# A decode kernel's output path: rows replicated over 32 partitions, halves merged by a predicated copy, and a finer last weight load

## The chip, the cores and the metric

The kernel runs on one core of one Trainium2 chip. The metric is device time in microseconds (us). A kernel is compared only with runs of the kernel before on the same chip in the same rounds. Engines are named as in the profile: PE (matmul), PEld (weight load), DVE (VectorE), ACT (ScalarE), POOL (GpSimd), SP (the queue that issues nearly all DMAs).

Two measures must be kept apart when reading on. A *time* (402.97 us) is the device's own, a *span* (401.6 us) is from the first to the last instruction of the one profiled execution.

## The reference, cut to what matters

One token is decoded. Part A is attention with 32 query heads over 4 key and value heads with 65,536 cached positions each. Part B is an MLP with four weight matrices. Both add to the same 1024 outputs.

```python
x  = A_x                                   # (1, 1, 1024), bf16
xn = _layernorm(x)
return x + _A_ref(xn, k_cache, v_cache, wq, wo) + _B_ref(xn, w1, w2, w3, w4)
# _A_ref: softmax(q k^T) v over 65536 positions, then @ wo
# _B_ref: ... h2 = gelu(layernorm(x1) @ w3) @ w4   (w4 is 3584 x 1024); x1 + h2
```

The caches and the weights are 170 MB, each byte is read once, and there is little to compute on each.

## The kernel before

SBUF is allocated in order of declaration. The small tensors come first, then four large ones: `W`, `Kn` and `Vn` receive the DMAs, `X` receives DVE transposes.

```python
orow = sb("orow", [P, 256], BF)            # output row, 512 bytes a partition
W  = sb("W",  [P, 14336], BF)              # weights
X  = sb("X",  [P, 2, 8192], BF)            # transposed K, written by DVE, read by PE
Kn = sb("Kn", [P, 2, 16384], BF)           # K cache, wq, at the end w4
Vn = sb("Vn", [P, 2, 16384], BF)           # V cache, wq, a part of wo
```

The output is summed in one PSUM tile. Its 1024 columns lie as four segments of 256 on partitions 0, 32, 64 and 96. A stationary operand of one column gives one row per segment, and four matmuls at four tile positions run side by side (in the trace one takes up to 0.42 us, and sixteen together take 1.02 us).

```python
def out_rows(items, reads, last=False):
    fns = []
    for lhs, rhs in items:                 # one weight row each
        for jj in range(4):
            fns.append(lambda e, ...: e.matmul(
                OUT_ps[32 * jj:32 * jj + 1, 0:256], lhs, rhs[:, 256 * jj:256 * jj + 256],
                start=False, stop=last, tile_position=(0, 32 * jj), ...))
    _grp(q_pe, fns, reads=reads, writes=[b_OUT], partial=True)
```

`_grp` makes PE wait for whoever wrote `OUT_ps` last. At the end the weight w4 arrives in four parts. Each entry is first row, number of rows, slot and offset; a row is 2 KB on each of 128 partitions.

```python
w4_parts = [(0, 14, 0, 0), (14, 8, 1, 0), (22, 4, 1, 8), (26, 2, 0, 14)]
...
for i in range(len(w4_parts)):
    w4_pe(i)                               # waits for part i, then 4 matmuls a row
_op(q_dve, lambda e: e.tensor_copy(orow[:, :], OUT_ps[:, 0:256]), ...)
ev_out = _dma(q_sp, ..., out=out[0, 0, :].rearrange("(j n) -> j n", j=4), in_=orow[0:97:32, :])
```

## Time and profile before

| Quantity | Value |
|---|---|
| time, median | 402.97 us |
| span of the profiled execution | 401.6 us |
| DMA | 170.20 MB at 424 GB/s, busy 0.9 or more in 38 of 40 slices |
| DVE, PE busy | 57%, 47% |
| last weight data packet ends | 398.39 us |
| last landing (completion of the last load) | 398.76 us |
| last output matmul ends | 399.42 us |
| store issued, span ends | 399.90 us, 401.59 us |

These lines of the page of the kernel before give the DMA's busy share in tenths and its rate over 40 slices, then its packets.

```profile
DMA  8999999999999999999999999999999999999995
GB/s 353 431 416 433 447 421 419 447 436 421 441 441 420 419 441 437 424 434 436 428 426 444 436 421 428 442 434 427 424 450 418 439 441 424 421 428 431 437 420 217
DMA packets 7088, 170.20 MB, mean 424 GB/s; under 512 B 916, under 2 KB 920, under 8 KB 1048
```

The DMA engines never rest until the last slice. Work on PE, DVE, ACT or POOL costs nothing while the stream hides it.

The chain of waits of the kernel before, at its end (start in us, duration in us, what):

```profile
374.88 23.88 DMA Kn<-in_B_w_dram
398.76 0.04 issue
398.80 0.62 PE OUT_ps L391 x7
399.42 0.02 issue
399.45 0.42 DVE orow L618
```

The timeline of the same stretch (start, duration, engine, line, operation, count, and in brackets the idle time before it and what ended it):

```profile
397.58 1.02 PE L391 MATMUL OUT_ps<-Kn,gh_bf 128*1 128x256 bf16 x16 [0.50 <-DMA Kn<-in_B_w_dram]
398.80 0.60 PE L391 MATMUL OUT_ps<-Kn,gh_bf 128*1 128x256 bf16 x8 [0.20 <-DMA Kn<-in_B_w_dram]
399.45 0.42 DVE L618 CAST orow<-OUT_ps 128x256 bf16<-128x256 f32 x1 [11.34 <-PE OUT_ps L391]
399.90 0.65 SPq L619 DMA_DIRECT2D out_dram<-orow  x1
```

PE begins the last eight matmuls 0.04 us after the last landing. From there it is a chain of latencies to the end of the span.

### The profile page before, as it was taken

To read this page: it belongs to the slowest core of one execution; us is meant where nothing else is said; L and a number is where in the kernel's file an instruction comes from. 1 tells how busy PE (TensorE), PEld (TensorE's weight loads), DVE (VectorE), ACT (ScalarE), POOL (GpSimd) and SP (SyncE) were. 2 spreads that over 40 slices of the span, in tenths; PEclk is the share of its full clock that TensorE was granted. 3 is DMA by queue.
4 is the path that set the end of the run, shared out by engine and by line. 5 is a ranking of instruction groups with operands and counts; after the bars stand their busy time and mean duration, and the time that the engine had idled before them with its cause. 6 is when DMAs were issued, how large, how long until landed. Compare 5 with 4: busy or idle time off the path is not lost.

```text
span 401.6 us, 5142 instructions
## 1 busy us (share of the span) xinstructions
PE 187.7 (47%) x2043; PEld 84.2 (21%) x2059; DVE 227.8 (57%) x400; ACT 48.4 (12%) x127; POOL 62.0 (15%) x90
## 2 busy tenths in 40 slices
PE   0361445064525745275630966353433545344674
PEld 0250111021103511062110731121111311111142
DVE  0217666277806588255753387676836775778410
ACT  0000211011101011011110011111201111112100
POOL 5000013011211011110310102111110102122110
PEclk9999999999855565555565555665565855656556
DMA  8999999999999999999999999999999999999995
GB/s 353 431 416 433 447 421 419 447 436 421 441 441 420 419 441 437 424 434 436 428 426 444 436 421 428 442 434 427 424 450 418 439 441 424 421 428 431 437 420 217
DMA packets 7088, 170.20 MB, mean 424 GB/s; under 512 B 916, under 2 KB 920, under 8 KB 1048
## 3 DMA queue, kind: packets, MB, share of 16 engines
q1 hardware_dynamic: 6920, 169.87, 98.4%
q8 instruction: 16, 0.26, 0.2%
q14 instruction: 8, 0.07, 0.0%
q10 hardware_dynamic: 144, 0.00, 0.0%
HBM read 169.87 MB, written 0.00 MB: 423 GB/s over the span
## 4 chain that ended last, share of the span: by engine, by line
DMA 54%; DVE 24%; PE 17%; issue 2%; ACT 2%; another core or an unknown queue 1%; SPq 0%; POOL 0%; ACTq 0%
DMA Kn<-in_A_k_cache_dram 43%; DVE X L463 12%; DMA Kn<-in_B_w_dram 6%; DMA Vn<-in_A_wq_dram 5%; PE H_ps L366 4%; DVE pT_f L516 3%; PE S_ps L475 3%; PE OT_ps L523 3%; DVE mrow L482 3%; PE M_ps L366 2%; ACT p_sb L505 2%; PE PT_ps L514 1%; PE M_ps L551 1%; PE OUT_ps L391 1%; DVE Yall L380 1%
## 5 line engine op out<-in xcount | busy, mean ns | idle before, releaser
L463 DVE STREAM_TRANSPOSE X<-Kn 128x1024 f32<-128x1024 f32 x128 | 151.7, 1215 | 64.5 <-DMA Kn<-in_A_k_cache_dram 64.5
L523 PE MATMUL OT_ps<-Vn,pT_f 128*32 128x512 bf16 x512 | 59.9, 620 | 54.1 <-DVE pT_f L516 54.1
L475 PE MATMUL S_ps<-X,Yall 128*32 128x512 bf16 x512 | 58.0, 598 | 17.0 <-DVE X L463 17.0
L488 PE MATMUL MB_ps<-Rm,Lmat 128*128 128x16 bf16 x32 | 6.2, 193 | 87.7 <-DVE Rm L483 87.7
L537 POOL TENSOR_TENSOR O_acc<-O_acc,tmpO 128x513 f32<-128x513 f32 x28 | 32.9, 1176 | 89.1 <-ACT tmpO L531 89.1
L535 POOL TENSOR_SCALAR O_acc<-O_acc,ff 128x513 f32<-128x513 f32 x28 | 19.6, 700 | 150.7 <-ACT ff L510 150.7
L505 ACT ACTIVATE p_sb<-S_ps,brun 128x512 bf16<-128x512 f32 x32 | 22.0, 688 | 173.1 <-DVE brun L503 154.6
L482 DVE TENSOR_REDUCE mrow<-S_ps 128x1 f32<-128x512 f32 x32 | 21.6, 674 | 24.6 <-PE S_ps L475 24.6
L531 ACT ACTIVATE tmpO<-OT_ps 128x512 f32<-128x512 f32 x32 | 19.2, 598 | 107.8 <-PE OT_ps L523 107.8
L475 PEld LDWEIGHTS S_ps<-X,Yall 128*32 128x32 bf16 x512 | 16.5, 126 | 54.7 <-DVE X L463 38.6
L516 DVE STREAM_TRANSPOSE pT_f<-PT_ps 128x512 f32<-128x512 f32 x32 | 22.9, 716 | 7.8 <-PE PT_ps L514 4.2
L523 PEld LDWEIGHTS OT_ps<-Vn,pT_f 128*32 128x32 bf16 x512 | 14.6, 128 | 59.4 <-DVE pT_f L516 42.7
L488 PEld LDWEIGHTS MB_ps<-Rm,Lmat 128*128 128x128 bf16 x32 | 3.3, 103 | 112.2 <-DVE Rm L483 112.2
L514 PE MATMUL PT_ps<-p_sb,permR 128*128 128x512 bf16 x16 | 9.5, 594 | 21.2 <-ACT p_sb L505 21.2
L366 PEld LDWEIGHTS H_ps<-xn_bf,W 128*128 128x128 bf16 x224 | 14.4, 172 | 1.7 <-issue 1.7
L366 PE MATMUL H_ps<-xn_bf,W 128*128 128x1 bf16 x224 | 14.5, 202 | 0.0
L514 PEld LDWEIGHTS PT_ps<-p_sb,permR 128*128 128x128 bf16 x32 | 3.4, 106 | 42.4 <-ACT p_sb L505 42.4
L492 DVE TENSOR_REDUCE Bst<-MB_ps 128x1 f32<-128x16 f32 x32 | 5.6, 174 | 8.3 <-PE MB_ps L488 8.3
L330 PE MATMUL M_ps<-ln_s,ones_f 128*128 128x1 f32 x6 | 1.8, 362 | 17.5 <-DVE ln_s L329 17.5
L533 POOL COPY O_acc<-tmpO 128x513 f32<-128x513 f32 x4 | 2.5, 615 | 47.5 <-ACT tmpO L531 47.5
L551 PE MATMUL M_ps<-O_acc,cb_W 128*128 128x128 f32 x32 | 7.4, 403 | 2.0 <-DVE cb_W L544 2.0
L391 PE MATMUL OUT_ps<-Kn,gh_bf 128*1 128x256 bf16 x112 | 5.8, 370 | 3.5 <-DMA Kn<-in_B_w_dram 3.5
(101 smaller groups left out, 114.0 us busy)
## 6 DMA issues: line engine op xcount, KB each, us to landing
Kn<-in_A_k_cache_dram SPq DMA_DIRECT2D x15, 4096.0 KB, 27.4
Vn<-in_A_v_cache_dram SPq DMA_DIRECT2D x15, 4096.0 KB, 22.3
W<-in_B_w_dram SPq DMA_DIRECT2D x2, 3584.0 KB, 25.1
W<-in_A_wo_dram SPq DMA_DIRECT2D x3, 2048.0 KB, 23.2
Kn<-in_A_wq_dram SPq DMA_DIRECT2D x1, 4096.0 KB, 12.3
Vn<-in_A_wq_dram SPq DMA_DIRECT2D x1, 4096.0 KB, 21.4
W<-in_B_w_dram SPq DMA_DIRECT2D x2, 2048.0 KB, 32.2
Kn<-in_A_k_cache_dram SPq DMA_DIRECT2D x2, 2048.0 KB, 24.8
```

The costliest lines, as they stand in the source:

```text
L366: fns.append(lambda e, j=j, cx=cx: e.matmul(ps_tile[:, c0 + cx:c0 + cx + 1], lhs_fn(j - j0, cx), rhs_fn(j), start=(j == 0 and cx == 0), st ...
L463: _op(q_dve, lambda e, ix=ix: e.transpose(out=X32[:, xs, 1024 * ix:1024 * (ix + 1)], in_=Kn32[:, s, 4096 * half + 1024 * ix:4096 * half + ...
L475: fns.append(lambda e, we=we, cm=cm, mv=mv: e.matmul(S_ps[32 * cm:32 * cm + 32, :], Yall[:, h, we, :, :].rearrange("p a g -> p (a g)"), mv ...
L482: _op(q_dve, lambda e: e.reduce_max(mrow[:, m:m + 1], S_ps[:, :], axis=AX.X), reads=[b_S], writes=[b_mrow[m]])
L505: _op(q_act, lambda e: e.activation(p_sb[:, m, :], S_ps[:, :], ACTF.Exp, bias=brun[:, kn:kn + 1], scale=SCALE, accum_out=tmpO[:, m, 512:513]),
L514: _op(q_pe, lambda e: e.matmul(PT_ps[:, :], permR[:, :], p_sb[:, m, :], start=True, stop=True), reads=[b_p[m], b_const], writes=[b_PT])
L516: _op(q_dve, lambda e: e.transpose(out=pT_f[:, :], in_=PT_ps[:, :]), reads=[b_PT], writes=[b_pT])
L523: fns.append(lambda e, q=q, q4=q4: e.matmul(OT_ps[32 * q4:32 * q4 + 32, :], pT_bf[:, q, :, 1], Vn[:, s, 8192 * half + 512 * q:8192 * half ...
L531: _op(q_act, lambda e: e.activation(tmpO[:, m, 0:512], OT_ps[:, :], ACTF.Copy), reads=[b_OT], writes=[b_tmpO[m]], partial=True)
L535: _op(q_pool, lambda e: e.tensor_scalar(out=O_acc[:, :], in0=O_acc[:, :], scalar1=ff[:, m:m + 1], scalar2=0.0, op0=ALU.mult, op1=ALU.add), ...
L537: _op(q_pool, lambda e: e.tensor_tensor(out=O_acc[:, :], in0=O_acc[:, :], in1=tmpO[:, m, :], op=ALU.add), reads=[b_tmpO[m]], writes=[b_Oacc])
L551: fns.append(lambda e, t=t: e.matmul(M0_ps[:, 128:256], cb_W[:, t, :, :].rearrange("p g i -> p (g i)"), O_acc[:, t * P:(t + 1) * P], start ...
```

## The change

The change is meant to shorten that tail. Loading the last two weight rows one by one should leave four matmuls behind the last landing, not eight. A stationary operand broadcast to 32 columns puts each output segment on all 32 partitions of its quadrant. Then partitions 0 to 15 can keep the first 128 columns of a segment and partitions 16 to 31 the second 128, by a plain copy and a predicated copy, and the store has eight rows of 256 bytes in place of four of 512.

```diff
-        orow = sb("orow", [P, 256], BF)
+        orow = sb("orow", [P, 128], BF)
+        omask = sb("omask", [P, 1], F32)
...
+        _op(q_dve, lambda e: e.reduce_sum(omask[:, 0:1], sel16[...][:, :, 2:4], axis=AX.XY), ...)
...
-   OUT_ps[32 * jj:32 * jj + 1, 0:256], lhs, rhs[:, 256 * jj:256 * jj + 256],
+   OUT_ps[32 * jj:32 * jj + 32, 0:256], lhs.broadcast_to([P, 32]), rhs[:, 256 * jj:256 * jj + 256],
...                                        # the same in out_resid
-        w4_parts = [(0, 14, 0, 0), (14, 8, 1, 0), (22, 4, 1, 8), (26, 2, 0, 14)]
+        w4_parts = [(0, 14, 0, 0), (14, 8, 1, 0), (22, 4, 1, 8), (26, 1, 0, 14), (27, 1, 0, 15)]
...
-        _op(q_dve, lambda e: e.tensor_copy(orow[:, :], OUT_ps[:, 0:256]), ...)
-        ev_out = _dma(..., out=out[0, 0, :].rearrange("(j n) -> j n", j=4), in_=orow[0:97:32, :])
+        _op(q_dve, lambda e: e.tensor_copy(orow[:, :], OUT_ps[:, 0:128]), ...)
+        _op(q_dve, lambda e: e.copy_predicated(orow[:, :], omask[:].bitcast(uint32)..., OUT_ps[:, 128:256]), ...)
+        ev_out = _dma(..., out=out[0, 0, :].rearrange("(j n) -> j n", j=8), in_=orow[0:113:16, :])
```

`orow` shrinks by 256 bytes a partition and `omask` takes 32, since the allocator starts each tensor at a multiple of 32. In the built programs `W` starts at byte 36608 (143 x 256) before and at 36384 (142 x 256 + 32) after. The others follow at whole multiples of 256, so all four end up 32 bytes past a multiple of 256.

## The prediction

> **What bounds the kernel now.** DMA. The page's slices give a DMA busy share of 0.9 in 38 of 40 slices, 170.2 MB at 424 GB/s, against DVE 57% and PE 47% of a span of 401.6 us. Only what follows the last weight landing, or slows the DMA stream, can move the time. The chain of waits ends: DMA of the last weight rows to 398.76; eight matmuls 398.80 to 399.42 (0.62 us); the eviction of the output, 128x256, 0.42 us, to 399.87; issue of the store 399.90 (0.65 us); end of span 401.6. The trace's packets show the last two-row part as 128 packets of 4 KB, 0.159 us each, the last ending at 398.39, 0.4 us before PE starts; the store's four 512-byte packets take 0.026 us each and start 1.25 us after its issue. So the tail is latency, not bytes.
>
> **What the change does.**
> 1. Two one-row loads in place of a two-row load. Only 4 matmuls, not 8, follow the last landing. In the timeline 16 matmuls take 1.02 us and 8 take 0.60, so 4 fewer save 0.2 us. Packets become 2 KB. Packet durations are 1.213 us at 32 KB, 0.309 at 8 KB, 0.159 at 4 KB: about 0.008 us fixed each, so eight more packets on each engine cost 0.07 us. The extra issue on the SP queue (0.4 us, at 375) is 23 us early: free.
> 2. Output on 32 rows per quadrant: stationary operand 128x32 instead of 128x1. The trace has both: LDWEIGHTS 128x32 take 0.126 us (mean, scores line), 128x1 up to 0.128 us; matmul time follows the moving columns. 0. The Trainium skill ("TensorE: Matmul & The Clock Gate", section "LDWEIGHTS") says load time grows with the columns; the trace does not show it at this size.
> 3. Eviction in two halves. Fixed part plus 1.04 ns per column gives 0.29 us for 128 columns (a 128x128 DVE op on PSUM: 0.29 us). The predicated copy is estimated the same, up to 0.4. With 0.03 us between them: 0.61 against 0.42, +0.2 us.
> 4. Store as eight 256-byte rows. The data part was 0.026 us; halving it saves 0.01 us. The skill ("DMA: Bandwidth & Descriptors", section "Specifications") puts line rate at 512 B and more, with read-modify-write below; no run here shows it yet. 0 to +0.2 us, estimate +0.05.
> 5. The mask: one small reduction, about 0.17 us on DVE near 15 us, hidden behind the weight load.
> 6. Side effect: the output row shrinks by 256 bytes a partition and the mask takes 32, so the big buffers start 224 bytes lower, from a multiple of 256 to 32 past one. If DMA writes then need a further beat or burst per packet (estimate 1 to 10 ns on each of some 324 packets' worth of 32 KB per engine) the whole stream lengthens by 0.3 to 3 us. I give this one chance in six.
>
> **Sum.** -0.2 + 0.07 + 0.2 + 0.05 = +0.1 us: gain on PE given back on DVE. Predicted 403.1 us, 402.5 to 404.0. Within 2%: 0.96; faster 0.01; slower 0.03.
>
> **What would show each step.** Step 1: last group of 4 matmuls near 0.4 us; last landing at most 0.1 us later; packets of 2 KB near 0.084 us. Step 2: the same time for 16 output matmuls (1.02 us). Step 3: cast near 0.29, predicated copy 0.29 to 0.4 us. Step 4: eight packets under 0.026 us; end of span about 1.7 us after the store's issue. Step 6: 32 KB packets still 1.213 us and 424 GB/s.
>
> **What would make it wrong.** Step 6 true; the read-modify-write of short rows costing more than 0.2 us; the predicated copy running much longer than a plain one; or a load's semaphores arriving so late that the one-row parts land no sooner.

## More of the kernel before

The stretches view of the kernel before, over the 320 us in which nothing but the stream counts, gives the busy time of each engine, then PE's granted clock, the DMA's busy share and GB/s:

```profile
20.00:340.00 320.00, 152.28 (x1652) 69.00 (x1667) 194.03 (x333) 41.00 (x107) 46.14 (x52) 0.68 1.00 432
```

The busy share is 1.00 and the rate 432 GB/s.

## The result, and the profile after

The time after is 405.98 us (405.86 to 406.35, 5 runs) against 402.97 us (402.86 to 403.31, 5 runs). The ratio is 1.0075, with a 95% interval of 1.0061 to 1.0089. It is a slowdown of 3.0 us clear of noise, and outside the predicted range. A ratio is the mean time of one kernel's fast runs over that of the other's of the same rounds, so it is not quite the ratio of the medians quoted.

The same lines of the page after:

```profile
DMA  8999999999999999999999999999999999999994
GB/s 360 418 416 449 424 419 447 428 416 447 431 415 436 439 421 429 429 431 429 430 434 431 429 434 424 429 431 430 428 431 431 432 428 431 419 420 434 431 420 163
DMA packets 7240, 170.20 MB, mean 421 GB/s; under 512 B 944, under 2 KB 944, under 8 KB 1200
```

The stretch from 20 to 340 us after:

```profile
20.00:340.00 320.00, 151.06 (x1651) 68.89 (x1666) 193.99 (x333) 40.83 (x107) 45.50 (x51) 0.63 1.00 430
```

The DMA engines are as busy as before but move 430 GB/s, not 432, in a stretch where the diff changes no load. PE's granted clock differs too (0.68 and 0.63), but PE waits for the stream.

The end of the chain of waits after:

```profile
375.82 24.19 DMA Kn<-in_B_w_dram
400.01 0.04 issue
400.05 1.07 PE OUT_ps L393 x16
401.12 0.14 issue
401.26 0.43 PE OUT_ps L393 x4
401.69 0.14 issue
401.82 0.43 PE OUT_ps L393 x4
402.25 0.02 issue
402.27 0.30 DVE orow L620
402.58 0.02 issue
402.60 0.29 DVE orow L621
```

The timeline after, for the same stretch:

```profile
400.05 1.04 PE L393 MATMUL OUT_ps<-Kn,gh_bf 128*32 128x256 bf16 x16 [0.61 <-DMA Kn<-in_B_w_dram]
401.26 0.41 PE L393 MATMUL OUT_ps<-Kn,gh_bf 128*32 128x256 bf16 x4 [0.17 <-PE OUT_ps L393]
401.82 0.40 PE L393 MATMUL OUT_ps<-Kn,gh_bf 128*32 128x256 bf16 x4 [0.16 <-PE OUT_ps L393]
402.60 0.29 DVE L621 CAST_PREDICATED orow<-omask,OUT_ps 128x128 bf16<-128x128 uint32 x1
402.92 0.72 SPq L623 DMA_DIRECT2D out_dram<-orow  x1
```

The last DMA on the chain is no longer the last load but the four-row part at 400.01. From there the chain runs through three PE groups. The last load's completion, read from the trace's semaphore events, was at 401.32, and its matmuls began only at 401.82, when the group before them had ended. Splitting the load made the tail PE-bound.

The trace also holds each DMA packet with its start, duration and size. Tabulated by size, median duration in ns with the commonest values and their counts:

```
                 before               after
 32768 B x4096   1213 (1213 x4022)    1216 (1216 x2006, 1224 x788, 1213 x406, 1215 x350, ...)
 28672 B x384    1062 (1062 x376)     1066 (1066 x205, 1073 x90, ...)
 16384 B x1424    611 (611 x1389)      614 (614 x791, 621 x297, ...)
 last rows        159 (4096 B, x128)    84.5 (2048 B, 84 x128, others 85 to 96)
 output           26 (512 B, x4)        15 (256 B, x8)
```

Before, nearly every packet of 32 KB takes exactly 1213 ns. After, most take 1 to 12 ns more. Packets of 28 KB and of 16 KB grow by the same few ns (3 to 11), so the addition goes with the packet and not with its bytes.

Two sums tell how far these records carry. The durations of all packets of 2 KB and more, added up and divided by the 16 engines, grow from 396.1 to 398.0 us. So the records hold about 2.0 of the 2.46 us by which the last packet ends later, 0.1 of it from the finer last rows. The completion of the last load is signalled by 16 semaphore events, spread over 3 to 4 us, and the end of the kernel waits for the latest. Their mean is less subject to chance than the latest one: it lies between 397.19 and 397.39 us in the kernel before and in all eight experiments with aligned DMA buffers, and at 399.38 us in the changed kernel. The remaining half microsecond or so is in the latest signal alone, which comes 0.68 us after the one before it (0.14 us in the kernel before, up to 0.65 us in the aligned experiments).

The difference of the spans (404.69 - 401.59 = 3.09 us), cut at events that both traces have:

| Stretch | before | after | difference |
|---|---|---|---|
| start to the end of the last weight packet | 398.39 | 400.85 | +2.46 |
| to the last landing | 0.37 | 0.47 | +0.10 |
| to the end of the last output matmul | 0.66 | 0.93 | +0.27 |
| to the issue of the store (eviction) | 0.48 | 0.67 | +0.19 |
| to the end of the span (store) | 1.69 | 1.77 | +0.08 |

### The profile page after: what moved, and what is told of

The parts are those of the page before. It is cut to its first block, busy times and chain, and to the rows that moved or that the text cites. A ratio compares the mean times of both kernels' runs of the same rounds, so it can differ in the third digit from the quotient of the medians.

```text
span 404.7 us, 5147 instructions
## 1 busy us (share of the span) xinstructions
PE 187.2 (46%) x2043; PEld 84.8 (21%) x2059; DVE 228.1 (56%) x402; ACT 48.4 (12%) x127; POOL 62.0 (15%) x90
## 4 chain that ended last, share of the span: by engine, by line
DMA 54%; DVE 24%; PE 17%; issue 2%; ACT 1%; another core or an unknown queue 1%; POOL 0%; SPq 0%; ACTq 0%
DMA Kn<-in_A_k_cache_dram 43%; DVE X L465 13%; DMA Kn<-in_B_w_dram 6%; DMA Vn<-in_A_wq_dram 5%; PE H_ps L368 4%; PE S_ps L477 3%; DVE pT_f L518 3%; PE OT_ps L525 3%; DVE mrow L484 3%; PE M_ps L368 2%; ACT p_sb L507 1%; PE OUT_ps L393 1%; PE PT_ps L516 1%; PE M_ps L553 1%; DVE Yall L382 1%
## 5 line engine op out<-in xcount | busy, mean ns | idle before, releaser
L465 DVE STREAM_TRANSPOSE X<-Kn 128x1024 f32<-128x1024 f32 x128 | 151.7, 1215 | 65.7 <-DMA Kn<-in_A_k_cache_dram 65.7
L393 PE MATMUL OUT_ps<-Kn,gh_bf 128*32 128x256 bf16 x112 | 6.9, 415 | 4.9 <-DMA Kn<-in_B_w_dram 4.5
```

Of the source, the lines that this page charges most:

```text
L393: fns.append(lambda e, lhs=lhs, rhs=rhs, jj=jj: e.matmul(OUT_ps[32 * jj:32 * jj + 32, 0:256], lhs.broadcast_to([P, 32]), rhs[:, 256 * jj:2 ...
L465: _op(q_dve, lambda e, ix=ix: e.transpose(out=X32[:, xs, 1024 * ix:1024 * (ix + 1)], in_=Kn32[:, s, 4096 * half + 1024 * ix:4096 * half + ...
```

## The experiments

Two theories were set against each other. **A**: the new start address of the big buffers makes DMA writes slower, a fixed few ns on every packet, and that is the 2.4 us of the stream. **B**: the tail made the whole loss, and the longer packets belong to that one run. A third, **C**, concerns the tail alone: the wait of an output group for the group before it turns the split load from a gain into a loss. Twelve kernels ran, with five rounds each. All gave correct results. The kernel before measured 403.01, 402.98 and 402.88 us in the three calls (9 runs each).

### Only the start address

```diff
+        pad0 = sb("pad0", [P, 16], BF)    # 32 unused bytes, the kernel before otherwise
         W = sb("W", [P, 14336], BF)
```

> The kernel before, with 32 unused bytes a partition put in front of the big buffers, so that W, X, Kn and Vn start 32 bytes past a multiple of 256 as in the changed kernel; nothing else differs. Theory A (start address): the packets take the changed kernel's durations (1.214 to 1.225 us at 32 KB where 1.213 was the rule), the last weight packet ends about 2.4 us later, and the time is 405.0 to 405.8 us. Rival B (tail: the split load, the two-step eviction and the short rows make the whole loss, and the longer packets are a chance of that run): 402.9 to 403.3 us and packets of 1.213 us.

Measured: 405.46 us (405.40 to 405.64) against 403.01; ratio 1.0062 (1.0049 to 1.0075). The last data packet ended at 401.06 us, and the mean of the 16 last signals is 399.33 us. The packets took the durations of the changed kernel almost count for count: 1216 ns x2022, 1224 x797, 1213 x391 at 32 KB. The rate in the same stretch, from the stretches view of this kernel:

```profile
20.00:340.00 320.00, 157.33 (x1653) 68.11 (x1650) 194.08 (x333) 40.71 (x107) 45.38 (x51) 0.78 1.00 430
```

The end of its chain of waits:

```profile
377.20 24.31 DMA Kn<-in_B_w_dram
401.52 0.04 issue
401.56 0.62 PE OUT_ps L392 x8
402.19 0.02 issue
402.21 0.43 DVE orow L619
```

The tail is that of the kernel before, piece by piece (0.04, 0.62, 0.02, 0.43), and it begins 2.76 us later. Thirty-two unused bytes are enough for four fifths of the loss. Rival B falls. PE's mean granted clock was higher here than in the profile of before (0.752 and 0.677) and the kernel slower all the same, so PE's clock is not the cause.

### The change, realigned

```diff
         omask = sb("omask", [P, 1], F32)
+        pad0 = sb("pad0", [P, 112], BF)   # 224 unused bytes, the changed kernel otherwise
         W = sb("W", [P, 14336], BF)
```

> The changed kernel with 224 unused bytes a partition put back in front of the big buffers, so that they start where they did before. Theory A: packets back at 1.213 us, last data packet back near 398.4 to 398.5 us, and what remains is the tail, about 0.6 us: 403.4 to 403.8 us. Rival B: 405.7 to 406.3 us.

Measured: 403.68 us (403.27 to 403.79); ratio 1.0014 (1.0000 to 1.0027). Packets of 32 KB are back at 1213 ns (x4034), and all 256 packets of 2 KB take 84 ns. The stream is back too, and the end of the timeline is that of the changed kernel, 2.2 us earlier:

```profile
20.00:340.00 320.00, 159.40 (x1678) 69.33 (x1675) 194.07 (x333) 41.01 (x107) 46.71 (x52) 0.64 1.00 432
```

```profile
397.86 1.04 PE L394 MATMUL OUT_ps<-Kn,gh_bf 128*32 128x256 bf16 x16 [1.37 <-DMA Kn<-in_B_w_dram]
399.07 0.41 PE L394 MATMUL OUT_ps<-Kn,gh_bf 128*32 128x256 bf16 x4 [0.17 <-PE OUT_ps L394]
399.63 0.41 PE L394 MATMUL OUT_ps<-Kn,gh_bf 128*32 128x256 bf16 x4 [0.16 <-PE OUT_ps L394]
```

The last data packet ended at 398.74 us. What is left of the 3.0 us is 0.67 us. In the profile most of that is the tail: the span is 0.89 us longer than before, 0.53 us of it after the last data packet. The other 0.36 us is a later last packet, within the scatter of that packet among the aligned kernels (see below).

### Only the split load

```diff
-        w4_parts = [(0, 14, 0, 0), (14, 8, 1, 0), (22, 4, 1, 8), (26, 2, 0, 14)]
+        w4_parts = [(0, 14, 0, 0), (14, 8, 1, 0), (22, 4, 1, 8), (26, 1, 0, 14), (27, 1, 0, 15)]
```

> The kernel before with the last two weight rows loaded one by one, all else unchanged and aligned. Theory of the prediction: 0.2 us less work after the last landing, 402.9 us. Theory C, from the changed kernel's timeline: each output group waits for the one before it (0.14 to 0.17 us idle between groups) and the one-row groups queue behind the four-row group, so the last group ends about 0.9 us after the last landing instead of 0.66: 403.2 to 403.4 us.

Measured: 403.40 us (402.96 to 403.48) against 403.01; ratio 1.0007 (0.9994 to 1.0020). The median lies where theory C put it, but the interval holds no change. The timeline says more:

```profile
397.76 1.02 PE L391 MATMUL OUT_ps<-Kn,gh_bf 128*1 128x256 bf16 x16 [0.56 <-DMA Kn<-in_B_w_dram]
398.94 0.28 PE L391 MATMUL OUT_ps<-Kn,gh_bf 128*1 128x256 bf16 x4 [0.17 <-PE OUT_ps L391]
399.39 0.28 PE L391 MATMUL OUT_ps<-Kn,gh_bf 128*1 128x256 bf16 x4 [0.16 <-PE OUT_ps L391]
```

The last landing was at 398.95, the last group began at 399.39. The bracket names PE itself as what ended each wait, 0.16 to 0.17 us after the group before. In this profile the last two groups were lucky: PE's granted clock was 1.00 from 399.0 on, against 0.50 in the four other tails looked at (before, changed, realigned, output path alone), so four matmuls took 0.28 us and not 0.41. By the timeline the last group still ended 0.72 us after the last landing (399.39 + 0.28 - 398.95), against 0.64 before (398.80 + 0.60 - 398.76).

### Only the output path

The edit is the diff of the change without its line of `w4_parts`, with the padding of 224 bytes.

> The changed kernel's output path (32 rows, two-step eviction, eight 256-byte rows) with the two-row load of before and the buffers realigned. From the two profiles: the eviction takes 0.62 instead of 0.42 us, the store's issue 0.72 instead of 0.65 and the store ends at most 0.1 us later: 403.2 to 403.4 us, no change of packets or of the last landing. If short rows cost a read-modify-write of their own: over 403.6 us.

Measured: 403.05 us (402.92 to 403.34); ratio 1.0003 (0.9991 to 1.0016). The steps cost what was expected in the trace: cast 0.29 us, predicated copy 0.29 us, store issue 0.72 us, end of span 1.77 us after the issue. In this execution the last data packet ended 0.17 us earlier than in the profile of before (398.22), which hides most of it: that packet ends between 398.2 and 398.7 us in the aligned kernels, whatever their tail. So 0.2 us of eviction is seen in the timeline and not resolved in the times. A read-modify-write of its own for short rows is not seen.

### Other start addresses

The edit is that of the first experiment with `[P, 32]` (64 bytes) and `[P, 64]` (128 bytes).

> The kernel before with the big buffers 64 bytes past a multiple of 256. Theory A1 (the write side works in 256-byte pieces, so any start off 256 costs): packets of 1.214 to 1.225 us at 32 KB and 405.0 to 405.8 us, as at 32 bytes. Theory A2 (64-byte words): packets of 1.213 us and 402.8 to 403.3 us.

> The kernel before with the big buffers 128 bytes past a multiple of 256. Theory A1: 405.0 to 405.8 us. Theory A2, or one of 128-byte words: packets of 1.213 us and 402.8 to 403.3 us.

Measured: 404.90 us (ratio 1.0049, 1.0036 to 1.0061) and 404.76 us (1.0046, 1.0034 to 1.0059), against 402.98. Packets of 32 KB: 1215 ns x1846, 1222 x729 and 1213 x665 at 64 bytes; 1213 x1400, 1218 x817, 1221 x536 and others at 128. Both lose, so the words of 64 and of 128 bytes (A2) fall: a start at a multiple of 128 is not enough. They lose less than 32 bytes does (1.9 and 1.8 us against 2.4), and the times came out just under the expected range. The means of the 16 last signals agree: 398.94 and 398.75 us, against 399.33 at 32 bytes and at most 397.39 when aligned. What makes the rest of the difference stays open.

### The mask behind the buffers

```diff
-        omask = sb("omask", [P, 1], F32)
         W = sb("W", [P, 14336], BF)
...
         Vn = sb("Vn", [P, 2, 16384], BF)
+        omask = sb("omask", [P, 1], F32)
```

> The changed kernel with the four-byte mask allocated behind the big buffers instead of in front of them, nothing else: the buffers then start at a multiple of 512 (256 past one in the kernel before). Theory A: packets of 1.213 us and 403.3 to 403.8 us, as when it was realigned with padding. If a multiple of 512 were better than one of 256, packets shorter than 1.213 us and less than 403.2 us.

Measured: 403.62 us (403.43 to 403.93) against 402.98; ratio 1.0017 (1.0003 to 1.0031). Packets of 32 KB: 1213 ns x4040. Moving one declaration undoes the large part of the loss, with no padding. The buffers now start at a multiple of 512, which is no better than a multiple of 256.

### Control: only X off the boundary

`X` was declared last, behind 32 bytes of padding; `W`, `Kn` and `Vn` start at multiples of 256.

> Control: the kernel before with only X, which no DMA writes but DVE writes and PE reads, 32 bytes past a multiple of 256, and W, Kn and Vn at multiples of 256. Theory A (it is the DMA's writes): packets of 1.213 us, 402.8 to 403.3 us. If misaligned engine reads and writes took part: longer DVE transposes or matmuls (1.215 and 0.598 us before) and some of the 2.4 us.

Measured: 402.92 us (402.79 to 403.24); ratio 1.0000 (0.9987 to 1.0012). Packets of 32 KB: 1213 ns x4035. The groups view of this kernel shows DVE's writes into the shifted `X` and PE's reads of it:

```profile
L464 DVE STREAM_TRANSPOSE X<-Kn 128x1024 f32<-128x1024 f32 x128 | 151.7, 1215 | 63.5 <-DMA Kn<-in_A_k_cache_dram 63.5
L476 PE MATMUL S_ps<-X,Yall 128*32 128x512 bf16 x512 | 58.3, 601 | 17.0 <-DVE X L464 17.0
```

A transpose takes 1215 ns, as before (1215 ns). A matmul takes 601 ns, against 598 before, and 590 to 608 in the other runs; PE waits for the stream in any case. So DVE's writes into `X` and PE's reads of it do not carry the loss. The engines' reads of `W`, `Kn` and `Vn` had no control of their own, but with all four buffers shifted (first experiment) the transposes that read `Kn` took 1216 ns and the matmuls that read `Vn` 619 ns (620 before), while the DMA's share stayed at 1.00 and its packets were longer. What is left is where the DMAs write.

### Only Vn off the boundary

```diff
+        pad0 = sb("pad0", [P, 16], BF)
         Vn = sb("Vn", [P, 2, 16384], BF)
```

> Only Vn starts 32 bytes past a multiple of 256; W, X and Kn stay aligned. Vn takes all V loads, half of wq and a quarter of wo: 74 of 170 MB. Theory A (per packet, by destination): half of the 4096 packets of 32 KB (those into Vn, 2048) get longer and the rest stay at 1.213 us, with about 0.43 of the 2.4 us: 403.9 to 404.3 us. If one misaligned buffer were enough to slow the stream: 405 us and more.

Measured: 403.68 us (403.50 to 403.81) against 402.88; ratio 1.0020 (1.0007 to 1.0032). The loss is 0.8 us, 403.68 us where 403.9 to 404.3 were expected: a third of the loss of all buffers for 43% of the bytes. The mean of the 16 last signals moves less still, to 397.62 us, 0.2 to 0.4 us later than in the aligned kernels. The other half of the expectation missed: 2048 packets of 32 KB go into `Vn`, and yet 3727 of 4096 still show 1213 ns. The packet records are not a count of misaligned packets. The first experiment has a hint of the same: its first three transfers, to about 31 us, show 1213 ns although they are misaligned too. A backlog behind the recorded packets, which must fill before the record shows it and which aligned transfers in between drain, would fit both. No run here shows it, and it stays open.

### The wait between output groups

```diff
-            _grp(q_pe, fns, reads=reads, writes=[b_OUT], partial=True)
+            _deps(q_pe, reads, [])
+            for sv, vv in b_OUT.w.items():
+                if sv is not q_pe.sem:     # wait for the other engines only
+                    q_pe.wait((sv, vv))
+            _grp(q_pe, fns, reads=[], writes=[], partial=True)
+            _done((q_pe.sem, q_pe.cnt), reads, [b_OUT], partial=True)
```

The edit was applied to the split load on the kernel before, and to the realigned change.

> The one-row loads on the aligned kernel before, and the output groups no longer wait for the group before them on their own engine. Theory C: the 0.14 to 0.17 us between groups goes, the last group ends about 0.5 us after the last landing instead of 0.75, and the time is 402.8 to 403.2 us: the split no longer loses but wins next to nothing.

Measured: 402.81 us (402.64 to 402.88) against 402.88; ratio 0.9998 (0.9985 to 1.0010). The timeline of its last groups:

```profile
397.80 1.59 PE L391 MATMUL OUT_ps<-Kn,gh_bf 128*1 128x256 bf16 x24 [0.55 <-DMA Kn<-in_B_w_dram]
399.45 0.42 DVE L624 CAST orow<-OUT_ps 128x256 bf16<-128x256 f32 x1 [12.92 <-PE OUT_ps L391]
```

The three groups (16, 4 and 4 matmuls) are now one unbroken run. It ends at 399.39, 0.41 us after the last landing at 398.98 (0.64 before). Theory C holds in the timeline. The times of this kernel and of the one before do not differ clear of noise.

> The changed kernel, realigned with padding, without the wait of an output group for the one before. Theory C: 0.3 us less than realigned alone (403.68 us): 403.2 to 403.5 us; what is left over the kernel before is the two-step eviction (0.2 us).

Measured: 402.98 us (402.90 to 403.49) against 402.88; ratio 1.0005 (0.9993 to 1.0018). The gain over the realigned change is larger than expected, about 0.6 us after subtracting the kernel before (0.67 - 0.10). The trace accounts for 0.5 of it: by the timeline the last matmul ends 0.45 us after the last landing (398.81), against 0.96 us in the realigned change (landing 399.08, end 400.04). The intervals of their ratios overlap, so it is the timeline that shows the gain.

### An attempt to beat both

```diff
-        w4_parts = [(0, 14, 0, 0), (14, 8, 1, 0), (22, 4, 1, 8), (26, 2, 0, 14)]
+        w4_parts = [(0, 14, 0, 0), (14, 8, 1, 0), (22, 3, 1, 8), (25, 2, 0, 14), (27, 1, 1, 11)]
```

On the kernel before, with the edit of the groups above.

> An attempt to beat both: kernel before, aligned, no self-wait, the last six weight rows loaded as 3, 2 and 1 instead of 4 and 2, so that each output group is done when the next rows land. Expected: last group ends 0.35 to 0.45 us after the last landing instead of 0.66: 402.6 to 402.9 us, at the limit of what five rounds resolve; the timeline decides.

Measured: 402.75 us (402.69 to 402.95) against 402.88; ratio 0.9999 (0.9986 to 1.0013). The last group ends 0.42 us after the last landing (landing 398.81, matmuls of 0.99 us from 398.24), against 0.64 before. Some 0.2 us are gone from the tail, and five rounds do not resolve it. This is no version that beats the kernel before; it only equals it.

## Why the prediction was wrong, point by point

**What bounds the kernel.** Right. The stream of DMA bounds it, and the loss is mostly a loss of the stream.

**Step 6, the start address: the step that failed.** The prediction named the mechanism and its size, 1 to 10 ns a packet and 0.3 to 3 us, but gave it "one chance in six" and left it out of the sum. The 1 to 10 ns were worked out from no figure of the trace, so it is in part luck that the loss fell into a range whose ends differ by a factor of ten. The runs put it at 2.45 us (the kernel before with the shift alone) or 2.3 us (the change, minus the change realigned: 3.01 - 0.67). The commonest additions are 3 and 11 ns a packet. Of the Trainium skill's page on DMA the prediction drew only on what bears on step 4. The same page ("DMA: Bandwidth & Descriptors", section "How a descriptor splits into AXI transactions") says that a trn2 descriptor is split into transactions of 256 bytes, and that for one which does not start at a multiple of 256 the first transaction starts at the boundary below, and the bytes before the start are fetched unused. The page states the start rule for reads. The shifted buffers are what the DMA writes, and the sources did not move. The runs agree with a 256-byte rule on that side: offsets of 32, 64 and 128 lose, the two starts at multiples of 256 do not. That an extra transaction is what takes the few ns was not shown.

**Step 1, the split load: wrong in sign.** "Only 4 matmuls, not 8, follow the last landing" assumed that PE is free when the last row lands. It is not. The four-row group takes 1.04 us and the two landings after it came 0.66 and 1.31 us behind its own (400.01, 400.67, 401.32 in the changed kernel). With the wait of 0.16 us between groups PE falls behind, and the last group begins 0.5 us after its data landed. In place of -0.2 us on PE, the stretch from the last landing to the last matmul took +0.27 us in the changed kernel. With the wait between groups removed, the last group ended 0.41 us after the landing instead of 0.64, a gain of 0.23 us in one profile of each, which the times do not resolve (ratio 0.9998, 0.9985 to 1.0010): the predicted gain was there, behind a wait that the prediction did not read. The bracketed idle time in the timeline before, "DMA", named only the releaser that came last. The term for 2 KB packets was right: 84 ns predicted and measured in the realigned kernel. Its 0.07 us on the stream is not resolved: the last packet ends between 398.47 and 398.74 us in the six aligned kernels with a finer last load, and between 398.22 and 398.52 us in the three without.

**Step 2, the 32-column operand.** Right in its effect. Sixteen output matmuls take 1.04 us, against 1.02. In the instructions of the output tile a weight load of 128x32 takes 150 ns where one of 128x1 took 128 ns at most. So the load does grow with the columns, as the skill says, by too little to matter. The prediction's "the trace does not show it" is a misreading: it set the mean of one group (126 ns for 128x32) against the maximum of another (128 ns for 128x1). In that same trace the loads of 128x32 run from 93 to 151 ns and those of 128x1 from 79 to 128 ns.

**Step 3, eviction in two halves.** Right: 0.29 and 0.29 us, and 0.19 us more from the last matmul to the store.

**Step 4, the short rows.** Right: 15 ns a packet instead of 26, 0.08 us more from issue to end, of which the issue itself is 0.07. The skill's read-modify-write under 512 bytes left no cost that these runs can see.

**Step 5, the mask.** Right: 0.15 us at 16.9 us, on nobody's chain.

**The sum.** The predicted +0.1 us was -0.2 + 0.07 + 0.2 + 0.05. Measured, the tail is about +0.6 to 0.7 us (realigned against before; the interval of the ratio reaches from 0 to 1.1 us), by the timelines because step 1 turned, and the address adds 2.3 to 2.5 us.

## What to carry to other kernels

When a kernel is bound by its DMA stream, look at what a change does to the start addresses of the buffers that the stream writes, even if it touches only a small tensor declared in front of them: here 32 bytes cost more than every intended step together, and declaring the small tensor last cured it. Compare the packet durations of the two traces, since a few ns on each of thousands of packets hardly show in the GB/s of a slice. And before cutting the last load finer, check that the engine which consumes it is idle when it lands, and that no wait of its own stands between the groups.

## What the Trainium skill lacked or had wrong

- "DMA: Bandwidth & Descriptors", section "How a descriptor splits into AXI transactions", gives the start rule for what is read. It does not say that a destination in SBUF that starts off a multiple of 256 costs time: 3 to 11 ns on most packets of 16 to 32 KB, 2.45 us of 403 us (ratio 1.0062) at 32 bytes past, 1.9 us at 64 and 1.8 us at 128.
- "SBUF — State Buffer", section "Operand start alignment", says itself that it is about legality and that its runs timed nothing. Moving `X`, which DVE writes and PE reads, by 32 bytes changed nothing (ratio 1.0000); moving what DMAs write did.
- "DMA: Bandwidth & Descriptors", section "Specifications", has a read-modify-write for transfers under 512 bytes. Eight rows of 256 bytes took 15 ns each and the store ended 0.08 us later than four rows of 512 bytes; no further cost was seen.
- No page that was consulted tells why at 32 bytes past the boundary the first three transfers (to 31 us) keep 1213 ns, or why with `Vn` alone shifted 3727 of 4096 packets do, though the time grows by 0.8 us.
